# An FNet layer with an MLP on one core: the last step of the paired half, reordered

## The chip, the core and the metric

One NeuronCore of a Trainium2 chip runs the program. TensorE (PE) multiplies matrices into PSUM, VectorE (DVE), ScalarE (ACT) and GpSimd (POOL) work on vectors, and SyncE (SP) and GpSimd issue the transfers between HBM and the core's SBUF. The engines run side by side and wait for each other by semaphores; each works through its own instructions in the order in which the program gives them. The metric is the device time of one execution in microseconds (us): the median of the runs.

## The reference

```python
xn = _layernorm(x, axis=-1)                                   # x: 1 x 2048 x 640, float32
# _A_ref: real part of a DFT over the rows of a DFT over the columns
a = jnp.einsum("bsd,ed->bse", xn, dft_hid_re)
b = jnp.einsum("bsd,ed->bse", xn, dft_hid_im)
y = jnp.einsum("ts,bse->bte", dft_seq_re, a) - jnp.einsum("ts,bse->bte", dft_seq_im, b)
# _B_ref: w1 is 640 x 1536, w2 is 1536 x 640
h = _gelu(jnp.einsum("bsd,df->bsf", xn, w1) + b1)
m = jnp.einsum("bsf,fd->bsd", h, w2) + b2
return x + y + m
```

## The kernel before

All products are made in float32 out of two parts: a number is split into a high part (`high`, a copy on ACT) and a low part (`low`, a subtraction on DVE that needs the high part), and `product` issues three matmuls, high by high, high by low, low by high (lines 304 to 306). So a matmul needs both parts of what it reads, one from ACT and one from DVE.

The 2048 rows are four blocks of 512 (`NT` = 4). The MLP comes first. A *unit* is 128 of the 1536 hidden columns of one block: `hidden` (or, for two blocks at once, windows) sums it in a PSUM bank, `unit` applies the gelu, `split_unit` splits the result into a tile `hs`, and `output` multiplies it with w2 into five banks, 15 matmuls. Blocks 1 and 2 are done as a pair: `pair(k)`, k = 0 to 5, makes two units of each block by a Winograd-like scheme, in seven windows. Units of block 1 go on at once; those of block 2 are written to HBM (`gs`, from `keep`) and read back later (`load_unit`) into `units`, to be split and multiplied when block 2's turn comes. Two pairs of units, the last of blocks 1 and 2, are written out for later (`late_units`).

Beside each pair runs `beside_pair(k, at)`, called at seven places of the pair, in the order at = 2, 5, 6, 3, 8, 7, 4. It also turns the two matrices of the hidden DFT, wr and wi, into forms for a later stage, one chunk of 32 columns of each quarter at a time (five chunks, k = 1 to 5): `load_w` reads a chunk of both (SP), `turn_w` transposes it (DVE), and `prep_w(j, n)` forms it in three steps, n = 0, 1, 2 (`put_w`: high parts on ACT, low parts on DVE, additions on DVE, and a store `wit` on GpSimd for each form, eight stores in all). The raw chunk stands in places 0 and 1 of a four-row tile `row`, the turned one in places 2 and 3. The same four places take rows 12 to 15 of x (128 rows each, `load_x`), the fourth block's rows, for which the normalization is due: `ln_stats` (statistics on DVE), `ln_scale` (a root on ACT, five small operations on DVE), `ln_apply` (DVE). `put_z` then reorders the normalized rows by 16 transfers from SBUF to SBUF into a tile `z`, eight issued on SP and eight on GpSimd; `transpose_z` (DVE) and `prep_xt` (ACT, DVE) make of it the operand of block 3's hidden products.

After the last pair, block 2 is finished in a loop p = 2 to 11: in each turn up to p = 9 an `output` of 15 matmuls, the split of a unit that is used two turns on, and `between(p)`, the work beside it. From p = 10 on hidden products of block 3 come in. In `between`, `prep_w1` splits chunks of w1 for block 3, `load_w1` and `load_unit` read the next ones.

What sets the order is the program itself: it is written in order of each engine, by hand, and an engine that waits holds all that stands behind it in its queue. The places touched are in `beside_pair` for k = 5 (`LASTK`): `turn_w` at 6, `prep_w` steps at 3 and 7 (lines 1053 to 1061), `load_x` at 3 and 4, `split_unit` of units 0 and 1 at 7 and 4; and `between(2)` and `between(3)`, which hold the statistics, the scale, the applies and `put_z`. The seeds (`xab` from `banks`, line 1002 in the profile) are two sums of block 1 that ACT copies out of PSUM, into a place (`xab2`) that the last window of the pair reads before.

Of the kernel before, what the change touches and what calls it, by code (L numbers as in the profile page):

```python
# [27 lines left out]
def kernel(  # L28
# [55 lines left out]
    NF = F // P  # L84
# [104 lines left out]
    def high(h, s):  # L189
        nc.scalar.activation(h, s, AF.Copy)  # L190

    def low(l, s, h):
        nc.vector.tensor_tensor(l, s, h.bitcast(F32), op=ALU.subtract)  # L193
# [14 lines left out]
    def load_x(c, eng=nc.sync, k=None, home=None):  # L208

        slot[c] = c % NC if k is None else k  # L210
        xt[c] = (row_places if home is None else home)[:, slot[c]]
        eng.dma_start(xt[c], x[c * P : (c + 1) * P])

    def ln_stats(c):
        m = MV
        st = ST[1 if c == 0 else c % 2]
        half = D // 2
        for h in range(2):
            nc.vector.bn_stats(st[:, h, :], xt[c][:, h * half : (h + 1) * half])  # L219
        nc.vector.bn_aggr(m[:, slot[c], 0:2], st.rearrange("p a b -> p (a b)"))  # L220
# [37 lines left out]
    def zo_tile(name, shape=(P, NB, DQ), dtype=F32):  # L258
        return out_pool.tile(list(shape), dtype, tag="zo", bufs=1, name=name)
# [89 lines left out]
    def split_unit(g, a, fill=lambda k: None):  # L349
        hs = mr.tile([P, 2, TB], F32R, tag="hs", bufs=3, name=f"hs{g}")  # L350
        HT[g] = hs
        high(hs[:, 0], a)
        fill(1)
        low(hs[:, 1], a, hs[:, 0])
# [42 lines left out]
    def load_w(m, j):  # L397

        t = row_places[:, m].rearrange("p (e b) -> p e b", b=B)
        A["wraw", m] = t  # L400
        v = (wr, wi)[m].rearrange("(n r) d -> r n d", r=B)
        for q in range(Q):
            s0 = q * DQ + j * B
            nc.sync.dma_start(t[q * B : (q + 1) * B], v[:, :, s0 : s0 + B])
# [41 lines left out]
    def prep_w(j, k):  # L446

        (r1, r2, r4), (i1, i2, i4) = (
            (A["wt", m][:, : 2 * P], A["wt", m][:, 2 * P : 4 * P], A["wt", m][:, 4 * P :]) for m in range(2)
        )  # L450

        if k == 0:
            put_w(0, j, r1, r4)
            put_w(1, j, i1, i4)
            add(r4, r4, i4)
        if k == 1:
            put_w(6, j, i2, i4, True)
            add(i2, i2, r2)
            put_w(2, j, i2, r4)
            add(r2, r1, r2, ALU.subtract)  # L460
            add(r1, i2, r1, ALU.subtract)
            add(i1, i1, r1, ALU.subtract)
        if k == 2:
            put_w(3, j, r1)
            put_w(4, j, i1)
            put_w(5, j, r2)

    def add(dst, a, b, op=ALU.add):
        nc.vector.tensor_tensor(dst, a, b, op=op)  # L469
# [426 lines left out]
    def turn_x(key, z):  # L896
        transpose_z(key, Z[z], FORM_COLUMN[key[:2]] + int(key[2]))

    def split_x(key):
        split(*XF[key], zt.pop(key))  # L900
# [80 lines left out]
    def bias_sum(t, e):  # L981
        nc.scalar.activation(oacc[t][e], oacc[t][e], AF.Identity, bias=b2c[:, e : e + 1])

    def turn_sum(t, e, home=mr, tag="ab", biased=False):

        if not biased:
            bias_sum(t, e)
        yt = home.tile([P, TB], F32, tag=tag, bufs=2, name=f"ot{t}_{e}")
        nc.vector.transpose(yt, oacc[t][e])
        return yt  # L990

    def add_sum(t, e, yt):
        d = xo[t][:, :, e * B : (e + 1) * B]
        add(d, d, yt.rearrange("p (n i) -> p n i", i=B))

    def store_sums(t, *ks):
        for k in ks or range(len(YCOLS)):
            c0, c1 = YCOLS[k]
            nc.gpsimd.dma_start(ys[k][t], xo[t][:, :, c0:c1])
# [15 lines left out]
    LASTK = NF // 2 - 1  # L1015

    def beside_pair(k, at):

        if k == 0:

            if at == 5:
                bias_sum(0, 0)
                turn_x("t30", "a")
                turn_x("t31", "a")
                A["ot0"] = turn_sum(0, 0, rows, "yt", True)
                split_x("t30")
                split_x("t31")
            if at == 6:
                turn_x("t40", "a")
                turn_x("t41", "a")  # L1030
                split_x("t40")
                split_x("t41")
                bias_sum(0, 1)
                load_w(0, 0)
                load_w(1, 0)
            if at == 8:
                A["ot1"] = turn_sum(0, 1, rows, "yt", True)
            if at == 4:
                add_sum(0, 0, A["ot0"])
                add_sum(0, 1, A["ot1"])  # L1040
                store_sums(0, 0)
                bias_sum(0, 2)
            return
        j = k - 1
        if k == 1:
            if at == 2:
                add_sum(0, 2, turn_sum(0, 2, rows, "yt", True))
            if at == 5:
                finish(0, 3, 4)
                store_sums(0, 1, 2)  # L1050
            if at == 3:
                A["wst"] = zo_tile("wst", (P, NB * DQ), F32R)
        if at == (7 if k == 1 else 6):
            turn_w(0, j)
            turn_w(1, j)
        if k == 1:
            steps = {7: (0,), 4: (1,)}
        elif k == 2:
            steps = {5: (-1,), 7: (0, 1), 4: (2,)}
        elif k == LASTK:  # L1060
            steps = {3: (0,), 7: (1, 2)}
        else:
            steps = {3: (0,), 7: (1,), 4: (2,)}
        if at == (7 if k == 1 else 3) and j + 1 < ND:
            load_w(0, j + 1)
            load_w(1, j + 1)
        if k == LASTK and at == 3:
            load_x(12)
            load_x(13)
        for n in steps.get(at, ()):  # L1070
            prep_w(*((j - 1, 2) if n < 0 else (j, n)))
        if k == LASTK and at == 7:
            A["gs"] = place("xab3", (P, 5, TB), F32)
            for i in range(3, 6):
                load_unit(i)
            A["s1"] = place("xab2", (P, ND, TB), F32)
            split_unit(2 * NF, units[0])
        if k == LASTK and at == 2:
            for i in range(3):
                load_unit(i)  # L1080
        if k == LASTK and at == 4:
            load_x(14)
            load_x(15)
            for i in range(6, 8):
                load_unit(i)
            split_unit(2 * NF + 1, units[1])

    units = {}

# [66 lines left out]
    def between(p):  # L1156

        if p == 2:
            ln_stats(12)
            ln_stats(13)  # L1160
        if p == 3:
            ln_stats(14)
            ln_stats(15)
            ln_scale(NC)
            Z["z"] = zo_tile("z3")
            for c in range(3 * NC, 4 * NC):
                ln_apply(c)
            put_z(Z["z"], row_places, nc.gpsimd, nc.sync)
            new_xt(3)
        if p == 4:  # L1170
            with_bias(A["s1"][:, 0], 1, 2)
            keep_seed("x", A["s1"][:, :2])
        if p == 5:
            for e in range(2):
                less(A["s1"][:, 2 + e], 1, e, A["s1"][:, e])
            keep_seed("y", A["s1"][:, 2:4])
        for j in {6: (0,), 7: (1, 2), 8: (3, 4)}.get(p, ()):
            if j == 0:
                transpose_z("x30", Z["z"], 0)
            if j + 1 < ND:  # L1180
                transpose_z(f"x3{j + 1}", Z["z"], j + 1)
            prep_xt(f"x3{j}", j)
        if p == 10:
            open_place(*PLACES[3])
        if p == 11:
            open_place(*PLACES[2])
        for n in {2: (0,), 4: (1,), 5: (2,), 6: (3,), 7: (4,), 8: (5,), 9: (6, 7), 10: (8,), 11: (9,), 12: (10, 11)}.get(p, ()):
            prep_w1(AGAIN[n], 2 * NF + n)
            load_w1(2 * NF + 3 + n)
        if p in (2, 3):  # L1190
            load_unit({2: 8, 3: 9}[p])
        if p == 9:
            put_rows(3, row_places, nc.sync)
        if p == 10:
            A["s2"] = zo_tile("s2", (P, ND, TB))
            for k, key in ((0, "x"), (2, "us")):
                c0, c1 = SEEDS[key]
                nc.gpsimd.dma_start(A["s2"][:, k : k + c1 - c0], seeds[:, c0:c1])
# [57 lines left out]
    for p in range(2, 2 + NU):  # L1256
# [4 lines left out]
        elif p == NU + 1:  # L1261
# [3 lines left out]
            def fill(k):  # L1265
                for e in ((3,), (4, 2))[k]:
                    home, tag = (mr, "ab") if e == 2 else (rows, "yt")
                    kept[e] = with_bias(home.tile([P, TB], F32, tag=tag, bufs=2, name=f"s2_{e}"), 2, e)
# [691 lines left out]
```

## Time and profile before

| what | us |
|---|---|
| median of 3 runs | 857.02 (856.49 to 857.15) |
| the profiled execution | 856.42 |
| its span, first to last instruction | 854.6 |
| TensorE busy in it | 842.9 |
| VectorE busy | 685.9 |
| ScalarE busy | 372.0 |
| GpSimd busy | 80.7 |

A line of a timeline gives start, length, engine, line of the program, operation, out<-in by the program's names, shape and count; in brackets the idle time of the engine before it and what ended it. A line of stretches gives busy time by engine in one stretch, with the count of instructions, the granted clock of TensorE (1.00 is full), the share of time that the DMA engines were busy and what they moved. A line of DMA issues ends with the size in KB and the median time from issue to landing. TensorE's work is matmuls nearly throughout: the low digits of the page's slices are at its start and its end. The mean of a matmul there (387 to 390 ns) overlaps with the next, so the pace has to be read from starts. The last step of the pair, k = 5, lies between 181 and 200 us, and the loop over p follows it, to 245.

### The profile page before, as it was taken

The page shows a single profiled execution, that of the slowest core. Times are in us where ns is not written, and L with a number is a line of the kernel's source. Part 1 is how long each engine was busy: PE and PEld are TensorE (multiplying, and loading weights), DVE is VectorE, ACT ScalarE, POOL GpSimd, SP SyncE. Part 2 cuts the span into 40 slices and gives each one's busy share as a digit, 9 for nine tenths or more (in the row PEclk, how much of TensorE's full clock was granted, in tenths as well). Part 3 has the DMA queues.
Part 4 walks back from the last instruction along what each step waited for, and adds up shares of the span by engine and source line. Part 5 has one row for each costly group of instructions (what it writes and reads, how often), then busy time and mean ns, then how long its engine had stood idle before and what let it go on. Part 6 is the DMA issues. An engine that isn't in the chain of part 4 may idle for free.

```text
span 854.6 us, 10699 instructions
## 1 busy us (share of the span) xinstructions
PE 842.9 (99%) x3722; PEld 697.0 (82%) x3722; DVE 685.9 (80%) x912; ACT 372.0 (44%) x541; POOL 80.7 (9%) x147
## 2 busy tenths in 40 slices
PE   8999999999899999999999999999999999999998
PEld 7888888887688888888888888888888888888886
DVE  5979889757654778989898888889878888876895
ACT  6556657546254554534333343322324323244450
POOL 3340024223210000000000000000000000001012
PEclk9999999999999999999999999999999999999999
DMA  7995767878676959776843499474465899556353
GB/s 223 287 246 170 148 179 244 246 246 310 174 226 210 400 164 210 153 192 157 208 112 72 141 320 241 111 200 117 125 208 176 239 247 263 170 195 240 100 155 87
DMA packets 194054, 169.03 MB, mean 198 GB/s; under 512 B 57840, under 2 KB 164848, under 8 KB 193360
## 3 DMA queue, kind: packets, MB, share of 16 engines
q1 hardware_dynamic: 182528, 136.36, 60.4%
q0 software_dynamic: 9296, 31.47, 10.5%
q10 hardware_dynamic: 2176, 0.52, 0.3%
q8 instruction: 29, 0.48, 0.2%
q14 instruction: 25, 0.20, 0.1%
HBM read 117.71 MB, written 46.66 MB: 192 GB/s over the span
## 4 chain that ended last, share of the span: by engine, by line
PE 92%; issue 2%; DVE 2%; DMA 1%; ACT 1%; SPq 1%; POOL 1%; POOLq 0%; ACTq 0%
PE banks L305 27%; PE banks L306 27%; PE banks L304 27%; PE banks L326 10%; DMA g<-gs 1%; SPq L801 1%; DMA row<-in_A_x_dram 0%; POOL wit L444 0%; DVE st L219 0%; DVE hs L193 0%; DMA wit<-wst 0%; PE banks L707 0%; DVE row L469 0%; DVE row L235 0%; DVE xab L193 0%
## 5 line engine op out<-in xcount | busy, mean ns | idle before, releaser
L190 ACT ACTIVATE as<-r 128x1024 fp32r<-128x1024 f32 x80 | 85.0, 1062 | 170.3 <-PE banks L306 152.6
L306 PE MATMUL banks<-as,xab 128*128 128x512 f32 (+1 forms) x389 | 150.5, 387 | 0.0
L305 PE MATMUL banks<-as,xab 128*128 128x512 f32 (+1 forms) x389 | 150.5, 387 | 0.0
L304 PE MATMUL banks<-as,xab 128*128 128x512 f32 (+1 forms) x389 | 150.5, 387 | 0.0
L193 DVE TENSOR_TENSOR as<-r,as 128x1024 fp32r<-128x1024 f32 x80 | 97.1, 1215 | 38.1 <-ACT as L190 38.0
L304 PE MATMUL banks<-as,xc 128*128 128x512 f32 x234 | 91.0, 389 | 0.0
L305 PE MATMUL banks<-as,xc 128*128 128x512 f32 x234 | 91.0, 389 | 0.0
L306 PE MATMUL banks<-as,xc 128*128 128x512 f32 x234 | 91.0, 389 | 0.0
L304 PEld LDWEIGHTS banks<-as,xab 128*128 128x128 f32 x389 | 73.0, 188 | 14.9
L305 PEld LDWEIGHTS banks<-as,xab 128*128 128x128 f32 x389 | 73.0, 188 | 14.9
L306 PEld LDWEIGHTS banks<-as,xab 128*128 128x128 f32 x389 | 73.0, 188 | 14.8
L190 ACT ACTIVATE as<-rt 128x1024 fp32r<-128x1024 f32 (+1 forms) x36 | 36.5, 1015 | 78.1 <-PE banks L306 59.3
L326 PE MATMUL banks<-xt,xab 128*128 128x512 f32 x240 | 56.6, 390 | 0.0
L326 PEld LDWEIGHTS banks<-xt,xab 128*128 128x128 f32 x240 | 45.0, 188 | 9.3
L193 DVE TENSOR_TENSOR hs<-ab,hs 128x512 fp32r<-128x512 f32 x34 | 23.4, 688 | 35.3 <-ACT hs L190 34.8
L304 PEld LDWEIGHTS banks<-as,xc 128*128 128x128 f32 x234 | 43.9, 188 | 9.1
L305 PEld LDWEIGHTS banks<-as,xc 128*128 128x128 f32 x234 | 43.9, 188 | 9.1
L306 PEld LDWEIGHTS banks<-as,xc 128*128 128x128 f32 x234 | 43.9, 188 | 9.1
L193 DVE TENSOR_TENSOR as<-rt,as 128x1024 fp32r<-128x1024 f32 (+1 forms) x36 | 41.5, 1153 | 9.0 <-ACT as L190 9.0
L304 PE MATMUL banks<-hs,xc 128*128 128x512 f32 x120 | 46.8, 390 | 1.7 <-ACT hs L190 1.7
L305 PE MATMUL banks<-hs,xc 128*128 128x512 f32 x120 | 46.8, 390 | 0.2 <-DVE hs L193 0.2
L306 PE MATMUL banks<-hs,xc 128*128 128x512 f32 x120 | 46.7, 389 | 0.0
(301 smaller groups left out, 1678.6 us busy)
## 6 DMA issues: line engine op xcount, KB each, us to landing
raw<-in_A_dft_seq_re_dram SPq DMA_DIRECT2D x64, 256.0 KB, 5.3
raw<-in_A_dft_seq_im_dram SPq DMA_DIRECT2D x64, 256.0 KB, 5.2
w1r<-in_B_w_dram SPq DMA_DIRECT2D x144, 80.0 KB, 3.4
wit<-wst POOLq DMA_DIRECT2D x15, 384.0 KB, 4.3
wit<-wst POOLq DMA_DIRECT2D x20, 256.0 KB, 4.4
forms_ab<-xab SPq DMA_DIRECT2D x4, 1280.0 KB, 7.5
xab<-wit SPq DMA_DIRECT2D x13, 384.0 KB, 4.5
row<-xn SPq DMA_DIRECT2D x14, 320.0 KB, 5.1
```

The lines of the kernel that those rows point to most:

```text
L190: nc.scalar.activation(h, s, AF.Copy)
L193: nc.vector.tensor_tensor(l, s, h.bitcast(F32), op=ALU.subtract)
L304: nc.tensor.matmul(acc, wh, mh, start=first, stop=False, skip_group_check=goes_on)
L305: nc.tensor.matmul(acc, wh, ml, start=False, stop=False, skip_group_check=goes_on)
L306: nc.tensor.matmul(acc, wl, mh, start=False, stop=last, skip_group_check=goes_on)
L326: nc.tensor.matmul(acc, W1[i][:, a, j * P : (j + 1) * P], XT[j][:, b], start=n == 0, stop=n == len(steps) - 1)
L801: engines[q % len(engines)].dma_start(z[q * B : (q + 1) * B].rearrange("r (c a) d -> r a c d", a=NC)[:, a], rows[a * B : (a + 1) * B, :, q ...
```

## The change

In the last step of the pair the turn of the last chunk moves from place 6 to place 2, and the three steps of its forming from 3, 7, 7 to 5, 6, 3. Rows 12 and 13 are loaded at 5 instead of 3, rows 14 and 15 at 3 instead of 4, right behind the third step, which is the last to read their places. Unit 0 of block 2 is split at 3 instead of 7, unit 1 at 7 instead of 4. The statistics of rows 12 and 13 are taken at 8 and those of rows 14 and 15 at 4, both inside the pair, and no longer in `between(2)` and `between(3)`; the scale, the applies and the reordering come in `between(2)` instead of `between(3)`.

```diff
-        if at == (7 if k == 1 else 6):
+        if at == {1: 7, LASTK: 2}.get(k, 6):
             turn_w(0, j)
             turn_w(1, j)
...
         elif k == LASTK:
-            steps = {3: (0,), 7: (1, 2)}
+            steps = {5: (0,), 6: (1,), 3: (2,)}
...
-        if k == LASTK and at == 3:
+        if k == LASTK and at == 5:
             load_x(12)
             load_x(13)
         for n in steps.get(at, ()):
             prep_w(*((j - 1, 2) if n < 0 else (j, n)))
+        if k == LASTK and at == 3:
+            load_x(14)
+            load_x(15)
+            split_unit(2 * NF, units[0])
+        if k == LASTK and at == 8:
+            ln_stats(12)
+            ln_stats(13)
         if k == LASTK and at == 7:
             A["gs"] = place("xab3", (P, 5, TB), F32)
             for i in range(3, 6):
                 load_unit(i)
             A["s1"] = place("xab2", (P, ND, TB), F32)
-            split_unit(2 * NF, units[0])
+            split_unit(2 * NF + 1, units[1])
...
         if k == LASTK and at == 4:
-            load_x(14)
-            load_x(15)
             for i in range(6, 8):
                 load_unit(i)
-            split_unit(2 * NF + 1, units[1])
+            ln_stats(14)
+            ln_stats(15)
...
         if p == 2:
-            ln_stats(12)
-            ln_stats(13)
-        if p == 3:
-            ln_stats(14)
-            ln_stats(15)
             ln_scale(NC)
             Z["z"] = zo_tile("z3")
             for c in range(3 * NC, 4 * NC):
```

On DVE, from the third step of the forming on (`wst` is a form, `hs` a unit's split, `g` a unit read back, `zc` a unit of the pair, `st` and `mv` statistics), stands before:

```order
L193 TENSOR_TENSOR wst_4_1959<-row,wst_4_1959 128x256
L193 TENSOR_TENSOR wst_4_1963<-row,wst_4_1963 128x256
L193 TENSOR_TENSOR wst<-row,wst 128x256
L193 TENSOR_TENSOR hs_1975<-g_1863,hs_1975 128x512
L193 TENSOR_TENSOR hs_2009<-g_1865,hs_2009 128x512
L193 TENSOR_TENSOR hs_2030<-g_1867,hs_2030 128x512
L219 BN_STATS st_92<-row 128x6 x2
```

And in the change, at the same step:

```order
L469 TENSOR_TENSOR ab_1902<-ab_1902,banks 128x512
L193 TENSOR_TENSOR wst_4_1941<-row,wst_4_1941 128x256
L193 TENSOR_TENSOR wst_4_1945<-row,wst_4_1945 128x256
L193 TENSOR_TENSOR wst<-row,wst 128x256
L193 TENSOR_TENSOR hs_1954<-g_1865,hs_1954 128x512
L469 TENSOR_TENSOR zc_1880<-zc_1880,banks 128x512
L219 BN_STATS st_92<-row 128x6 x2
L220 BN_AGGR mv<-st_92 128x2
L219 BN_STATS st_93<-row 128x6 x2
L220 BN_AGGR mv<-st_93 128x2
L193 TENSOR_TENSOR hs_1986<-g_1867,hs_1986 128x512
```

The third step and the first unit's split (`hs_1954`) now stand ahead of the addition into `zc`, which stood between the first and the second step before, and the statistics of rows 12 and 13 stand ahead of the second unit's split.

A little further on DVE, around the applies (line 235), stands before:

```order
L193 TENSOR_TENSOR xab_2012<-w1r_1607,xab_2012 128x640
L193 TENSOR_TENSOR hs_2063<-xab_1970,hs_2063 128x512
L219 BN_STATS st_92<-row 128x6 x2
L220 BN_AGGR mv<-st_92 128x2
L219 BN_STATS st_93<-row 128x6 x2
L220 BN_AGGR mv<-st_93 128x2
L227 TENSOR_SCALAR mv<-mv 128x4
```

And in the change, with the unit that is used third (`hs_2042`) in front:

```order
L219 BN_STATS st_92<-row 128x6 x2
L220 BN_AGGR mv<-st_92 128x2
L219 BN_STATS st_93<-row 128x6 x2
L220 BN_AGGR mv<-st_93 128x2
L193 TENSOR_TENSOR hs_2042<-g_1869,hs_2042 128x512
L227 TENSOR_SCALAR mv<-mv 128x4
```

The w1 chunk and the fourth unit's split, which stood ahead of the statistics of rows 14 and 15, come behind the applies now.

On SP, from the units' loads on, stands before (x3 is three transfers in a row; `row` is rows 12 to 15, `z` the reordered rows, `w1r` a chunk of w1):

```order
L1094 DMA g_1867<-gs 128x512
L212 DMA row<-in_A_x_dram 128x640 x2
L1094 DMA xab_1970<-gs 128x512 x3
L212 DMA row<-in_A_x_dram 128x640 x2
L1094 DMA xab_1970<-gs 128x512 x2
L282 DMA w1r_2041<-in_B_w_dram 32x5x128 x4
L1094 DMA g_2046<-gs 128x512
L801 DMA z_2078<-row 32x4x160 x8
L1094 DMA g_2100<-gs 128x512
```

And in the change:

```order
L1100 DMA g_1869<-gs 128x512
L212 DMA row<-in_A_x_dram 128x640 x4
L1100 DMA xab_1981<-gs 128x512 x5
L801 DMA z_2051<-row 32x4x160 x8
L282 DMA w1r_2075<-in_B_w_dram 32x5x128 x4
L1100 DMA g_2080<-gs 128x512
L1100 DMA g_2100<-gs 128x512
```

All four rows now go ahead of the five unit loads into `xab`, and `z` goes ahead of one w1 chunk and one unit load.

## The prediction

> **What bounds the kernel now.** I read the page first, then the busy time by stretch, then TensorE's timeline in the two stretches where it is not full, then the lines of the other engines just ahead of those gaps.
>
> ```profile
> span 854.6 us, 10699 instructions
> PE 842.9 (99%) x3722; PEld 697.0 (82%) x3722; DVE 685.9 (80%) x912; ACT 372.0 (44%) x541; POOL 80.7 (9%) x147
> ```
>
> TensorE is the bound: 842.9 of 854.6 us. A change that leaves the matmuls as they are can gain only what TensorE loses by waiting or by a lower clock. The stretches show where that is (columns: length, PE busy with count, PEld, DVE, ACT, POOL, granted clock, DMA share, GB/s).
>
> ```profile
> 181.03:200.07 19.04, 19.04 (x85) 15.58 (x83) 9.50 (x23) 8.23 (x19) 6.25 (x13) 1.00 0.93 321
> 200.07:203.47 3.40, 1.44 (x5) 0.86 (x5) 2.38 (x6) 3.22 (x7) 2.52 (x6) 1.00 0.80 251
> 203.47:226.39 22.92, 22.92 (x102) 18.77 (x100) 14.28 (x32) 7.66 (x13) 6.44 (x12) 1.00 0.87 271
> 226.39:231.50 5.11, 1.73 (x7) 1.08 (x7) 4.49 (x7) 2.77 (x5) 0.00 (x0) 1.00 0.47 134
> 231.50:235.10 3.60, 3.60 (x10) 2.80 (x9) 3.57 (x7) 2.05 (x5) 0.00 (x0) 0.53 0.31 80
> 323.50:600.00 276.50, 276.50 (x1221) 228.96 (x1220) 241.75 (x221) 104.80 (x110) 0.00 (x0) 1.00 0.70 170
> ```
>
> The first row is the last step of the paired half (k = 5); TensorE is full in it. The last row gives the pace: 276.50 / 1221 = 0.2265 us for each matmul. In between are two holes, after 200.07 and after 226.39, and behind the second one the clock is at half (0.53). TensorE's own lines give their size:
>
> ```profile
> 198.03 0.39 PE L304 MATMUL banks<-as,w1f 128*128 128x512 f32 x1
> 199.84 0.39 PE L306 MATMUL banks<-xab,w1f 128*128 128x512 f32 x1
> 201.95 0.49 PE L304 MATMUL banks<-hs,xc 128*128 128x512 f32 x1 [1.73 <-ACT hs L190]
> 202.68 0.50 PE L305 MATMUL banks<-hs,xc 128*128 128x512 f32 x1 [0.23 <-DVE hs L193]
> 205.76 0.39 PE L306 MATMUL banks<-hs,xc 128*128 128x512 f32 x1
> 226.16 0.39 PE L306 MATMUL banks<-hs,r 128*128 128x512 f32 x1
> 229.49 0.49 PE L304 MATMUL banks<-hs,r 128*128 128x512 f32 x1 [2.93 <-ACT hs L190]
> 238.53 0.39 PE L306 MATMUL banks<-hs,r 128*128 128x512 f32 x1
> ```
>
> First hole: from 199.84 to 205.76 are 15 matmuls, 15 x 0.2265 = 3.40 us of work in 5.92, so 2.52 us lost. Second: from 226.16 to 238.53 are 30 matmuls, 6.80 us of work in 12.37, so 5.57 lost, the half clock included. Together 8.09 us. Both holes wait for a unit's split (`hs`: high part on ACT, low part on DVE).
>
> **First hole: what the change does to it.** The first output of block 2 needs unit 0 split. These lines of DVE and ACT carry it now:
>
> ```profile
> 187.12 0.85 DVE L409 STREAM_TRANSPOSE row<-row 128x640 f32<-128x640 f32 x1 [0.98 <-DMA row<-in_A_dft_hid_im_dram]
> 192.18 0.69 DVE L469 TENSOR_TENSOR ab<-ab,banks 128x512 f32<-128x512 f32 x1 [4.21 <-PE banks L306]
> 195.50 0.69 DVE L469 TENSOR_TENSOR zc<-zc,banks 128x512 f32<-128x512 f32 x1 [0.18 <-PE banks L306]
> 199.29 1.33 DVE L469 TENSOR_TENSOR row<-row 128x256 f32<-128x256 f32 x3
> 200.70 1.17 DVE L193 TENSOR_TENSOR wst<-row,wst 128x256 fp32r<-128x256 f32 x3
> 201.93 0.69 DVE L193 TENSOR_TENSOR hs<-g,hs 128x512 fp32r<-128x512 f32 x1
> 188.08 0.60 ACT L335 ACTIVATE ab<-banks 128x512 f32<-128x512 f32 x1 [0.82 <-PE banks L306]
> 192.90 0.72 ACT L346 ACTIVATE ab<-ab,b1c 128x512 f32<-128x512 f32 x1 [4.21 <-DVE ab L469]
> 193.53 1.11 ACT L190 ACTIVATE wst<-row 128x256 fp32r<-128x256 f32 x4
> 196.86 0.40 ACT L190 ACTIVATE wst<-row 128x256 fp32r<-128x256 f32 x1
> 200.25 1.13 ACT L190 ACTIVATE wst<-row 128x256 fp32r<-128x256 f32 x3 [1.34 <-issue]
> ```
>
> The second transposition stays where it is on DVE, behind the same add and the same landing: it ends at 187.97. DVE and ACT then sit idle (both 4.21) although the chunk lies ready. The change fills that hole. Behind 187.97 ACT has about two of the first step's four highs (half of 1.11) and the term (0.60): the second step starts at 189.1. Second step in before: from 196.86 to 199.29 + 1.33 = 200.62, 3.76 us; so its adds end at 192.9. The unit's add (0.69) is queued behind them on DVE: 193.5, some 0.7 later than now; its gelu (0.72): 194.3. Third step and split in before: from 200.25 to 201.93 + 0.69 = 202.62, 2.37 us; so unit 0 is split at 196.7, against 200.07 where TensorE wants it. **Gain 2.52**, cover 3.4.
>
> What is queued behind: the add into `zc` (195.50 now) goes behind the split's low part, 196.7 to 197.4. It frees the bank into which the last window starts at 198.03: 0.6 to spare, and TensorE does not wait unless the chain slips by more. Edits with one answer: the two transpositions, loads of rows 12 and 13 (behind the same three unit loads on SyncE) and the chunk's eight stores on GpSimd only go earlier; for these stores only the third step's last form waits, whose buffer is that of the first form: written out from about 189 on, wanted at about 195, and such a store takes 2.9 (first row of the next fence).
>
> **Second hole.** Here DVE waits for the reordered rows 12 to 15 (`z`), and the next split stands behind it in the queue.
>
> ```profile
> wit<-wst POOLq DMA_DIRECT2D x2, 384.0 KB, 2.9
> row<-in_A_x_dram SPq DMA_DIRECT2D x2, 320.0 KB, 4.9
> row<-in_A_x_dram SPq DMA_DIRECT2D x2, 320.0 KB, 6.9
> 208.72 0.88 DVE L219 BATCH_NORM_STATS2 st<-row 128x6 f32<-128x320 f32 x2
> 211.00 0.17 DVE L227 TENSOR_SCALAR mv<-mv 128x4 f32<-128x4 f32 x1
> 212.17 2.18 DVE L235 TENSOR_SCALAR row<-row,mv 128x640 f32<-128x640 f32 x4
> 201.81 1.25 ACT L1002 ACTIVATE xab<-banks,b2c 128x512 f32<-128x512 f32 x2
> 206.84 1.28 ACT L226 ACT_TABLE_LOAD   x1
> L801 SPq DMA_DIRECT2D z<-row x8: 593/673/1277, 214.4 to 219.6; - x8
> 226.91 1.30 DVE L263 STREAM_TRANSPOSE ztx<-z 128x512 f32<-128x512 f32 x2 [7.97 <-DMA g<-gs]
> 229.69 0.69 DVE L193 TENSOR_TENSOR hs<-xab,hs 128x512 fp32r<-128x512 f32 x1
> 233.54 0.69 DVE L193 TENSOR_TENSOR hs<-g,hs 128x512 fp32r<-128x512 f32 x1
> 228.82 0.61 ACT L190 ACTIVATE hs<-xab 128x512 fp32r<-128x512 f32 x1
> ```
>
> (The releaser is named `g`, the last landing near; the transposition reads `z`.) From the first `z` issue, 214.4, to the transposition, 226.91, are 12.5 us. Rows 14 and 15 go out when the third step has read their places, about 0.7 ahead of the split's end: 196.0, where the same step's lows end at 200.70 + 1.17 = 201.87 in before. By the two DMA rows (the loads of rows 12, 13, then of 14, 15) they land 4.9 to 6.9 later, 200.9 to 202.9. Statistics of two tiles take 211.00 - 208.72 = 2.3: those of 12 and 13 run from 197.4 to 199.7, unit 1's low part to 200.4, those of 14 and 15 end at 203.2 (early landing) to 204.1 (late: one tile is left), and unit 2's low part (0.7) at 203.9 to 204.8. ACT has its own chain: the two seeds (1.25) go into a place that the last window still reads, so from 200.1; a gelu 0.7, unit 2's high part 0.6 and the table load 1.28 bring it to 204.0, about the same. From 211.00 to the end of the applies, 212.17 + 2.18 = 214.35, are 3.35. So `z` starts at 207.4, **7.0 earlier**; the bounds are 207.2 and, with another us for the traffic, 209.
>
> With no first hole TensorE comes to the output that stalled at 200.07 + 7 x 3.40 = 223.87 (15 matmuls for each of seven outputs). Its split, moved by 7.0: high part 228.82 + 0.61 - 7.0 = 222.4 (1.4 to spare); low part 230.38 - 7.0 = 223.4, wanted with the second matmul at 224.1 (0.7 to spare). One output on, 227.27: low part 234.23 - 7.0 = 227.2, wanted at 227.5 (0.3). So the hole closes, by a small margin: **gain 5.57**. The cover is thin: from half a us of lateness on, each further us of `z` costs TensorE a us, and that sets the upper end.
>
> On SyncE's queue `z` now also goes ahead of the four pieces of one w1 chunk and one unit load. For `z` that can only help. The chunk is formed on ACT just ahead of the split whose output stalled, so a late chunk delays it as a late `z` does; I take nothing for it, since the chunk is issued right behind `z` and read after `z`'s first two transpositions (1.30) and a split; the bound is 1 us, and it lies in the same rival as late `z`.
>
> By the Trainium skill, "DMA: Bandwidth & Descriptors", Anatomy of one DMA (about 2 us and then 436 GB/s), an estimate for the 16 pieces of 80 KB is 4.9 us, and `z` would have 7 us to spare; the trace has 12.5 for it, and the trace decides.
>
> **Sum.** The profiled execution took 856.42 with a span of 854.6; 856.42 - 2.52 - 5.57 = 848.3. The median of the runs, 857.02, lies 0.6 above it: 848.9, and I forecast 849.0, as the margins at the second hole leave about 0.1. It is a floor too, since nothing else is freed.
>
> **Rivals.** *Late `z`.* For it: DMA share is 0.93 in the pair's stretch, and the stores moved forward there compete with rows 14 and 15 for it; margins are 0.3 to 0.7. If `z` takes 14 us, or starts at 209, TensorE waits 1 to 2.5 us: 850 to 851.5. A wait near 3 brings the half clock again (half of 3.6 us, 1.7): up to 853.6. The row shows no loss of clock behind the first hole's 1.73 and a loss behind 2.93. The skill's "TensorE: Matmul & The Clock Gate", Part 1, puts the fall behind an idle window of about 3.4 us; by that alone such a rest would cost only itself, 852.0.
>
> *Crowded pair.* The `zc` add slips past 198.03: say a first-step store holds the third step's buffer for 2 us more. Then the last window waits 1 to 2: 850 to 851. Against: 0.6 to spare, and 5 us of age for the store.
>
> *Slower.* DVE works in order: the statistics of rows 14 and 15 now stand ahead of unit 2's low part, which TensorE wants at 200.07 + 2 x 3.40 = 206.9. If row 15 lands late, that part is ready 1.9 behind the landing (a tile 1.15, the part 0.7), TensorE waits there, and the half clock adds 1.7; `z` is then covered by the wait itself. It eats the whole 8.09 and another 1.7 from a landing at 213 on, 17 us after the issue; at 215 the time is 857.0 - 8.1 + 10.0 + 1.7 = 860.6. The slowest such landing shown is 6.9.
>
> *Nothing.* Some other wait takes both places, for instance the seeds or the table load in front of block 2: 856 to 858. The columns of ACT (44% busy) speak against it.
>
> **Chances.** Both holes closed, within 0.7: 0.64. Late `z`: 0.22 without the half clock, 0.04 with it. Crowded pair: 0.05. Slower: 0.02. Nothing: 0.03. A change within 0.2% (1.7 us) can't be told from none here. So faster 0.95, same 0.03, slower 0.02. The range runs from 848.4 (the floor less 0.5, as the lowest of the runs, 856.49, lies 0.5 below their median) to 852.0, which holds the forecast, the crowded pair and nearly all of late `z`.
>
> **What would show it.** Right: TensorE full from 200.07 on, unit 0's low part at about 196.7, `zc` at 197, rows 14 and 15 issued near 196, `z` issued near 207.4, its transposition near 220, clock 1.00 throughout 226 to 235. Wrong: TensorE waiting for `zc` ahead of 200; a wait for `hs` at 224 or 227; the transposition's line later than 221; or DVE idle ahead of its statistics beyond 203.

## The result, and the profile after

The change takes 849.90 us, the median of six runs (849.36 to 851.72), beside 857.05 for the kernel before in the same rounds (856.49 to 858.62). The ratio is 0.9918, with a 95% interval of 0.9905 to 0.9931: 7.15 us faster. The profiled execution took 850.62, 0.7 above the median, with a span of 848.8. The page's first lines:

```profile
span 848.8 us, 10702 instructions
PE 841.9 (99%) x3722; PEld 696.3 (82%) x3722; DVE 686.3 (81%) x912; ACT 372.5 (44%) x541; POOL 80.8 (10%) x147
```

Every engine is busy about as long as before, and the span is 5.8 shorter: 4.8 of it are time in which TensorE was not busy (11.7 before, 6.9 now), the other 1.0 is its busy time, for the same 3722 matmuls. The stretches after, with the columns as before (length, PE, PEld, DVE, ACT, POOL, clock, DMA share, GB/s):

```profile
181.25:200.30 19.05, 19.05 (x85) 15.66 (x84) 12.68 (x31) 10.30 (x24) 8.66 (x16) 1.00 1.04 346
200.30:207.10 6.80, 6.80 (x32) 5.63 (x31) 3.98 (x11) 3.74 (x6) 1.08 (x2) 1.00 1.01 387
207.10:213.00 5.90, 5.20 (x23) 3.64 (x22) 5.76 (x14) 4.45 (x8) 2.14 (x4) 1.00 0.41 130
...
224.00:231.50 7.50, 7.34 (x32) 5.37 (x31) 7.34 (x12) 4.88 (x9) 0.89 (x2) 1.00 0.67 193
231.50:235.00 3.50, 3.50 (x17) 2.92 (x16) 2.30 (x4) 1.26 (x3) 0.20 (x1) 1.00 0.91 273
```

TensorE is full through 200, where the first hole was, and the clock is 1.00 in every row, the last one included, where it was 0.53 before: the half clock is gone. Two things are new. The pair's stretch and the one behind it have the DMA engines busy throughout (1.04 and 1.01, against 0.93 and then 0.80 to 0.87 before), and there is a small hole in the third row, where before had none. TensorE's starts show what is left, one matmul being due 0.2265 behind the other:

```profile
200.14 0.39 PE L306 MATMUL banks<-xab,w1f 128*128 128x512 f32 x1
200.37 0.39 PE L304 MATMUL banks<-hs,xc 128*128 128x512 f32 x1
...
207.17 0.39 PE L304 MATMUL banks<-hs,xc 128*128 128x512 f32 x1
207.62 0.50 PE L305 MATMUL banks<-hs,xc 128*128 128x512 f32 x1
...
210.93 0.39 PE L304 MATMUL banks<-hs,xc 128*128 128x512 f32 x1
211.95 0.50 PE L305 MATMUL banks<-hs,xc 128*128 128x512 f32 x1 [0.64 <-DVE hs L193]
...
225.46 0.39 PE L304 MATMUL banks<-hs,r 128*128 128x512 f32 x1
225.90 0.50 PE L305 MATMUL banks<-hs,r 128*128 128x512 f32 x1
...
229.25 0.39 PE L304 MATMUL banks<-hs,r 128*128 128x512 f32 x1
229.75 0.50 PE L305 MATMUL banks<-hs,r 128*128 128x512 f32 x1
```

From the last window (200.14) into block 2 (200.37) there is no gap. Four waits remain in this execution, each for a unit's low part on DVE: 0.22 at 207, 0.79 at 211, 0.21 and 0.27 at 225 and 229, with some 0.1 more behind each, 1.9 in all. The two holes of before had 8.1. In a second profiled execution of the same kernel (experiment 11) only the last two waits are there, so the first two are not a fixed part of the change.

DVE's lines say why the low parts at 207 and 211 were late:

```profile
187.83 0.85 DVE L409 STREAM_TRANSPOSE row<-row 128x640 f32<-128x640 f32 x1 [1.47 <-DMA row<-in_A_dft_hid_im_dram]
...
196.85 0.69 DVE L193 TENSOR_TENSOR hs<-g,hs 128x512 fp32r<-128x512 f32 x1
197.46 0.68 DVE L469 TENSOR_TENSOR zc<-zc,banks 128x512 f32<-128x512 f32 x1
201.16 0.89 DVE L219 BATCH_NORM_STATS2 st<-row 128x6 f32<-128x320 f32 x2 [1.98 <-DMA row<-in_A_x_dram]
203.96 0.89 DVE L219 BATCH_NORM_STATS2 st<-row 128x6 f32<-128x320 f32 x2 [1.11 <-DMA row<-in_A_x_dram]
205.84 0.89 DVE L219 BATCH_NORM_STATS2 st<-row 128x6 f32<-128x320 f32 x2 [0.75 <-DMA row<-in_A_x_dram]
206.89 0.68 DVE L193 TENSOR_TENSOR hs<-g,hs 128x512 fp32r<-128x512 f32 x1
208.38 2.18 DVE L235 TENSOR_SCALAR row<-row,mv 128x640 f32<-128x640 f32 x4
...
211.21 1.29 DVE L193 TENSOR_TENSOR hs<-xab,hs 128x512 fp32r<-128x512 f32 x2
222.33 1.30 DVE L263 STREAM_TRANSPOSE ztx<-z 128x512 f32<-128x512 f32 x2 [5.51 <-DMA w1r<-in_B_w_dram]
```

Three times DVE stands idle in front of statistics until a row has landed (1.98, 1.11, 0.75). The third unit's low part (206.89) is queued behind the last of them, the fourth's (211.21) behind the applies. The loads of the rows, among the issues between 189 and 199 (KB, us to landing):

```profile
row<-in_A_x_dram SPq DMA_DIRECT2D x4, 320.0 KB, 8.0
```

And who issues `z`, from the view of that tile (the last two figures are the first and the last issue):

```profile
L801 SPq DMA_DIRECT2D z<-row x8: 594/608/1432, 210.6 to 215.7; - x8
```

The four rows take 8.0 us from issue to landing, where the two pairs of loads in before took 4.9 and 6.9. `z` is issued at 210.6, 3.8 earlier than before.

### The profile page after: what moved, and what is told of

Read it like the earlier page. It is cut to its first block, busy times and chain, and to the rows that moved or that the text cites. A ratio compares the mean times of both kernels' runs of the same rounds, so it can differ in the third digit from the quotient of the medians.

```text
span 848.8 us, 10702 instructions
## 1 busy us (share of the span) xinstructions
PE 841.9 (99%) x3722; PEld 696.3 (82%) x3722; DVE 686.3 (81%) x912; ACT 372.5 (44%) x541; POOL 80.8 (10%) x147
## 4 chain that ended last, share of the span: by engine, by line
PE 93%; DMA 3%; issue 1%; SPq 1%; DVE 1%; POOL 1%; ACT 0%; POOLq 0%; ACTq 0%
PE banks L305 27%; PE banks L306 27%; PE banks L304 27%; PE banks L326 10%; DMA row<-in_A_x_dram 1%; PE banks L691 1%; DMA w1r<-in_B_w_dram 1%; DMA wit<-wst 1%; SPq L801 1%; POOL wit L444 0%; SPq L282 0%; PE banks L707 0%; DVE row L235 0%; DVE hs L193 0%; DVE st L219 0%
```

## The experiments

The theory: each of the two holes was a chain that came late, first the forming and unit 0's split, then rows, statistics and `z`; both chains are now early enough, and what is left comes from the rows, whose landing the busy DMA engines delay. Rivals: one of the parts does it all; the earlier stores are what slows the rows; or something else than the rows' time makes `z` late. Every kernel computes all of the reference and none leaves work out; two move more than they need: experiment 3 stores some forms twice, and experiment 12 copies 1 MB that nobody reads.

**1. The turn, the forming and the splits alone; rows and statistics as before.**

```diff
-        if k == LASTK and at == 5:
+        if k == LASTK and at == 3:
             load_x(12)
             load_x(13)
...
+            load_x(14)
+            load_x(15)
...
+            ln_stats(12)
+            ln_stats(13)
+        if p == 3:
+            ln_stats(14)
+            ln_stats(15)
```

> The kernel before with the turn, the forming and the splits of units 0 and 1 moved as in the change, rows 12 to 15 and their statistics as before. Theory: the two holes are in series and the second hangs on the landing of rows 14 and 15, not on TensorE. The first hole (2.5 us) closes, TensorE comes to the second that much sooner and waits that much longer unless z comes sooner as well: 857.0 if z is first issued at 214.4 as before, less by as much as it is issued sooner; I expect 212 to 214 and 854.5 to 857. Rival (the holes add up, each worth its own size): 854.5 with z issued at 214.4.

Measured: 855.59, ratio 0.9982 (0.9973 to 0.9992). TensorE's line at its second hole:

```profile
228.33 0.51 PE L304 MATMUL banks<-hs,r 128*128 128x512 f32 x1 [4.59 <-ACT hs L190]
```

The first hole is gone, and the second has grown: TensorE arrives 2.8 earlier (its last matmul starts at 223.35 instead of 226.16) and waits 4.59 where it waited 2.93. `z` itself is issued at 212.6 instead of 214.4, and its transposition comes 1.2 earlier (225.75 instead of 226.91). So of the 1.5 us that the kernel gains most is what `z` gained, and the closed hole of 2.5 by itself gives next to nothing. The gains of two holes in series are not independent: what the first gives, the second takes, until its own chain moves too.

This run also shows what the earlier stores do to the rows. Rows 12 and 13 are loaded where they were before (issues between 189 and 199), and what moved around them is the turn, the forming with its stores, and the splits:

```profile
row<-in_A_x_dram SPq DMA_DIRECT2D x2, 320.0 KB, 7.7
```

They took 4.9 in the kernel before. So the earlier stores are at least part of what makes the rows late.

**2. The change with the splits of units 0 and 1 at their old places.**

```diff
         if k == LASTK and at == 3:
...
-            split_unit(2 * NF, units[0])
...
         if k == LASTK and at == 7:
...
-            split_unit(2 * NF + 1, units[1])
+            split_unit(2 * NF, units[0])
...
         if k == LASTK and at == 4:
...
+            split_unit(2 * NF + 1, units[1])
```

> The change with the splits of units 0 and 1 left at their old places (7 and 4), so behind the statistics of rows 12 and 13 on VectorE. Theory: VectorE works in order and row 13 lands at 201.1, so unit 0's low part comes at about 202.2 and the first hole opens again with 2 to 2.5 us; z is issued near 210.6 as in the change, TensorE comes later to it and finds no wait there: 851 to 852. Rival (the earlier forming alone closes the first hole, since all its work is done by 197): 849.5 to 850.3.

Measured: 850.04, ratio 0.9916 (0.9901 to 0.9931): the same as the change. The time expected was missed. The wait did come back, as its lines on DVE and TensorE show:

```profile
199.70 0.89 DVE L219 BATCH_NORM_STATS2 st<-row 128x6 f32<-128x320 f32 x2 [1.09 <-DMA row<-in_A_x_dram]
200.75 0.64 DVE L193 TENSOR_TENSOR hs<-g,hs 128x512 fp32r<-128x512 f32 x1
...
201.45 0.50 PE L305 MATMUL banks<-hs,xc 128*128 128x512 f32 x1 [1.04 <-DVE hs L193]
```

Unit 0's low part stands behind row 13's statistics and TensorE waits 1.04. The waits at 207 and 211 are gone here, as they are in the second execution of the change, and those for `z` come to 0.6, read from TensorE's starts, where that execution had 1.4: TensorE comes there later. The earlier splits by themselves earn nothing that these runs show. The wait is paid at whichever split first stands behind rows that have not landed.

**3. The stores of the last chunk's first two steps issued twice, to load the DMA engines** (lines of the program from 446 on are one higher in this kernel).

```diff
-            nc.gpsimd.dma_start(wits[w][j][:, :, c0:c1], t.bitcast(F32))
+            for _ in range(2 if last and w in (0, 1, 2, 6) else 1):
+                nc.gpsimd.dma_start(wits[w][j][:, :, c0:c1], t.bitcast(F32))
```

> The change with the last chunk's stores of the first two steps' forms (five of eight, 1.5 MB) issued twice each. Theory: what is left of the second hole comes from rows 12 to 15 landing late (7 to 10 us after issue) beside these stores; twice the stores put the landing of row 15 some 3 to 4 us later, z is first issued at 213 to 215 and the time is 852 to 856. Rival (it comes from VectorE, which has the statistics in front of the splits): z at 210.6, 849.5 to 850.5.

Measured: 864.35, ratio 1.0084 (1.0068 to 1.0099), far more than expected, and by other ways:

```profile
199.37 0.42 ACT L190 ACTIVATE wst<-row 128x256 fp32r<-128x256 f32 x1 [5.11 <-DMA wit<-wst]
...
201.68 0.80 PE L304 MATMUL banks<-as,w1f 128*128 128x512 f32 x1 [3.64 <-DVE zc L470]
```

ACT waits 5.11 for the buffer that a store still reads, the add into `zc` behind it is late, and the last window waits 3.64: the crowded pair, as the prediction described it, at a price that the change itself does not pay (0.06 there). Later `z` waits too (first issued at 223.3), since its tile lies where some of those forms stood, and TensorE waits another 7.02, at 237.67, for the split that stands behind its transposition. As a test of the rows it says nothing: they were issued later, and their statistics, from 201.54 to 205.2, ended no later than in the change.

**4. The seeds' stores written later in the program** (the two calls of `keep_seed` moved to `p == 8`).

> The change with the two stores of seeds x and y (512 KB each) moved from p = 4 and 5 to p = 8, behind the transfers of z and out of their time. Theory: they share the DMA engines with the last pieces of z; without them z is transposed 10 us after its first issue instead of 11.7, the waits at 225 to 230 (0.7 us together) go: 849.0 to 849.4. Rival (z is bound by its own issue on SyncE, 6.5 us, and its small pieces): no difference, 849.9.

Measured: 849.97, ratio 0.9917 (0.9902 to 0.9932). This tested nothing: the stores are issued by GpSimd, and nothing else of GpSimd's stood between the old and the new place, so its order stayed the same and the stores still went out right behind its half of `z` (from 214.5). It serves as a second measurement of the change.

**5. The seeds' two stores on SyncE, at `p == 8`.** GpSimd issues these two stores of 512 KB right behind its half of `z`.

```diff
-            keep_seed("x", A["s1"][:, :2])
...
-            keep_seed("y", A["s1"][:, 2:4])
...
+        if p == 8:
+            for key, k in (("x", 0), ("y", 2)):
+                nc.sync.dma_start(seeds[:, SEEDS[key][0] : SEEDS[key][1]], A["s1"][:, k : k + 2])
```

> The change with the stores of seeds x and y issued on SyncE at p = 8, behind the loads of four w1 chunks there (the run before it, with these stores moved in the program alone, left GpSimd's own order as it was and so tested nothing). Theory: the two stores, 1 MB, take DMA time from the last pieces of z; without them z is transposed about 2 us sooner behind its first issue (9.5 to 10.5 instead of 11.7), and the waits at 225 to 230, 0.7 together, go: 849.0 to 849.5. Rival (z is bound by its own issue and pieces): 11.7 as before, 849.9.

Measured: 849.28 (848.89 to 849.78), ratio 0.9910 (0.9893 to 0.9926). Its issue of `z`:

```profile
L801 SPq DMA_DIRECT2D z<-row x8: 594/624/1377, 209.2 to 214.3; - x8
```

The transposition, on DVE's timeline:

```profile
217.66 1.30 DVE L263 STREAM_TRANSPOSE ztx<-z 128x512 f32<-128x512 f32 x2 [2.25 <-DMA w1r<-in_B_w_dram]
```

The releaser named is a load that landed close by, as in the change; the transposition reads `z`, which experiments 7, 9 and 10 name there.

And the stretch 196 to 236:

```profile
196.00:236.00 40.00, 40.00 (x178) 32.99 (x177) 27.12 (x53) 20.67 (x33) 7.71 (x15) 1.00 0.82 259
```

TensorE is busy in all 40.00 us, as it was in none of the kernels above. From the first issue of `z` to the transposition it is now 8.5, in the change 11.7; from its last issue (214.3, and 215.7 in the change) 3.4 and 6.6. So some 3 us of the time of `z` come from the seeds' stores beside its last pieces. The other profiles agree: wherever GpSimd issues these stores behind `z`, the transposition comes 11.7 to 13.2 behind the first issue, and 8.5 to 9.0 in the four kernels where it does not (experiments 5, 7, 9 and 10). The issues between 213.8 and 216.5 in the change show the neighbours (KB each, us to landing):

```profile
seeds<-xab POOLq DMA_DIRECT2D x2, 512.0 KB, 5.5
z<-row SPq DMA_DIRECT2D x4, 80.0 KB, 4.7
```

In the kernel of this experiment the same four pieces, the last that SyncE issues, took 3.7; the last two of them took 3.3, and 5.6 in the change. The time came out as expected, but its lead over the change, 0.6, is within the intervals.

**6. Rows 14 and 15 loaded from ACT's queue.**

```diff
-            load_x(14)
-            load_x(15)
             split_unit(2 * NF, units[0])
+            load_x(14, nc.scalar)
+            load_x(15, nc.scalar)
```

> The change with rows 14 and 15 loaded from ScalarE's own queue, right behind unit 0's high part, instead of SyncE's. Theory: what made z late (issued at 210.6, where 207.4 was forecast) is the landing of rows 14 and 15 at 203.9 and 205.8, held up in SyncE's queue behind the units and rows 12 and 13; on a queue of their own they land at 201 to 203, z is first issued at 208 to 209, the waits of units 2 and 3 at 207 and 211 (1.2 together) go and half of those at 225 to 230: 848.6 to 849.3. Rival (all DMA engines are full there, share 0.95 to 1.03, so another queue gains nothing): row 15 lands at 205 or later, 849.9.

Measured: 850.42 (849.37 to 850.57), ratio 0.9918 (0.9904 to 0.9933). No time is gained. The loads between 189 and 199 in its profile:

```profile
row<-in_A_x_dram ACTq DMA_DIRECT2D x2, 320.0 KB, 7.0
row<-in_A_x_dram SPq DMA_DIRECT2D x2, 320.0 KB, 7.9
```

This profile is of the fastest of its executions (849.37). A queue of their own saves these two rows at most 1 us out of 8, and in experiment 7, where they are loaded in the same way, they took 8.3. The waits at 207 and 211 are gone and those for `z` stay (0.44 at 224.62), but the second execution of the change shows the same without this edit. So at most a small part of the rows' 8 us is SyncE's queue.

**7. Experiments 5 and 6 together.**

> Both edits, rows 14 and 15 on ScalarE's queue and the two seeds on SyncE. Theory: no wait of TensorE is left between 198 and 240; the time is the floor, 848.0 to 848.9. Rival (each edit without effect): 849.9.

Measured: 849.20 (848.32 to 849.28), ratio 0.9904 (0.9890 to 0.9919). The time is above what was expected, and one wait is left (0.42, for unit 3's low part at 210.95). Not to be told from experiment 5: with the seeds out of the way the rows' queue gives nothing that can be seen.

**8. The change with the scale, the applies and `put_z` at their old place.** In `between`, `if p == 2:` is `if p == 3:` again for that block.

> The change with the scale, the applies and the reordering back at p = 3, the statistics as in the change. Theory: on VectorE a w1 chunk and unit 3's split come in front of the applies, and on SyncE a w1 chunk and a unit in front of z; z is first issued 1.5 to 2 us later (212 to 212.6); the wait for unit 3 at 211 (0.9) goes, and TensorE waits 2.5 to 3.5 us more for z: 851.4 to 852.6, more by 1.7 if the clock falls. Rival (the earlier statistics bring all of the gain, since the rows set the time): 849.5 to 850.3.

Measured: 853.23, ratio 0.9955 (0.9941 to 0.9970). Its issue of `z`:

```profile
L801 SPq DMA_DIRECT2D z<-row x8: 593/620/1352, 211.4 to 216.5; - x8
```

TensorE's two waits:

```profile
226.99 0.50 PE L304 MATMUL banks<-hs,r 128*128 128x512 f32 x1 [1.73 <-ACT hs L190]
227.93 0.50 PE L305 MATMUL banks<-hs,r 128*128 128x512 f32 x1 [0.44 <-DVE hs L193]
```

And the stretch of these waits, with the one behind it:

```profile
224.87:228.20 3.33, 1.16 (x4) 0.46 (x3) 3.23 (x6) 2.30 (x4) 0.00 (x0) 1.00 0.26 75
228.20:231.50 3.30, 3.30 (x9) 2.53 (x9) 3.27 (x6) 2.30 (x4) 0.00 (x0) 0.53 0.37 104
```

`z` is issued 0.8 us later than in the first profile of the change and 2.4 later than in its second (experiment 11), and its transposition, at 224.42, comes 2.1 and 3.0 later. That costs 3.3 us: 1.73 and 0.44 of waiting, and then the half clock (0.53), for which the expectation had allowed. The late-`z` rival is real, and the change stands only a little ahead of it.

**9. The kernel before, with only the seeds' stores moved to SyncE** (the edit of experiment 5 alone).

> The kernel before, with the seeds x and y stored from SyncE at p = 8 and nothing else. Theory: the second hole hangs on the landing of z alone, and the two stores take some 3 us of its time; z is issued at 214.4 as before and transposed 8.5 to 9 us later, at 223, ahead of 226.4 where TensorE wants the split: the second hole (5.5) goes, the first stays: 851.3 to 852.2. Rival (z has to start earlier, as in the change): 855 or more.

Measured: 851.90 (851.46 to 852.84), ratio 0.9940 (0.9928 to 0.9953). Its issue of `z`:

```profile
L801 SPq DMA_DIRECT2D z<-row x8: 593/702/1157, 213.8 to 219.2; - x8
```

The transposition on DVE, and TensorE at what is left of the second hole:

```profile
222.78 1.31 DVE L263 STREAM_TRANSPOSE ztx<-z 128x512 f32<-128x512 f32 x2 [4.43 <-DMA z<-row]
...
230.15 0.50 PE L305 MATMUL banks<-hs,r 128*128 128x512 f32 x1 [0.16 <-DVE hs L193]
```

`z` is issued 0.6 earlier than in before and transposed 4.1 earlier (222.78 instead of 226.91), so 3.5 of it belong to the stores. The first hole stays (1.73 at 201.50), the second one is all but gone. Beside the kernel before in the same rounds (856.74) the two stores moved give 4.84 us, where the whole reordering, run beside them in experiment 11, gives 6.80.

**10. Experiment 1 with the seeds' stores moved.**

> The turn, forming and splits moved as in the change, rows and statistics as before, the seeds x and y on SyncE at p = 8. Theory: the first hole goes by the early split; z, issued at 212.6 as in the run with the split alone and transposed 8.5 to 9 us later at 221.3, leaves a wait of 0 to 1.2 at 223.9: 849.2 to 850.5. Rival (the earlier rows and statistics are needed): 854 or more.

Measured: 850.75 (850.42 to 851.24), ratio 0.9926 (0.9913 to 0.9938), a little over what was expected, with `z` issued at 213.6, a us later than expected. Beside experiment 5 (849.28), the earlier rows, statistics and `z` are worth about 1.5 once the seeds are out of the way.

**11. The change once more**, beside the next kernel.

> The change as it is, beside the others on one chip: 849.5 to 850.5, rows 14 and 15 landing 7 to 9 us after issue, z issued at 209.5 to 211.

Measured: 849.94 (849.29 to 850.74), ratio 0.9916 (0.9903 to 0.9930). In its profile the rows take 7.6 and `z` goes out at 209.0, 1.6 earlier than in the first one: such a step varies by that much between executions of one kernel. TensorE does not wait at 207 and 211 here; what is left is the wait for `z`, transposed at 221.43:

```profile
224.95 0.50 PE L305 MATMUL banks<-hs,r 128*128 128x512 f32 x1 [0.43 <-DVE hs L193]
...
228.80 0.50 PE L305 MATMUL banks<-hs,r 128*128 128x512 f32 x1 [0.15 <-DVE hs L193]
```

Read from TensorE's starts, these two waits with what follows them come to 1.4 us.

**12. The change with 1 MB more to move:** a copy from HBM to HBM that nobody reads, issued by ACT in place 6 of the pair.

```diff
+    spare_rows = dram.tile([4, P, TB], F32, name="spare_rows")
...
+        if k == LASTK and at == 6:
+            nc.scalar.dma_start(spare_rows, gs[0:4])
```

> The change with one copy of 1 MB from HBM to HBM into a tensor that nobody reads, issued from ScalarE's own queue behind the second step of the forming, at about 192. Theory: the DMA engines are full from 189 to 207 (shares 0.95 to 1.03), so any other transfer puts off rows 14 and 15, by 2.5 to 5 us (1 MB read and written at some 390 GB/s); z is issued at 212 to 215 and the time is 851.5 to 855. Rival (the rows wait for their own queue, not for the engines): rows and time as in the change.

Measured: 853.97, ratio 0.9958 (0.9942 to 0.9974). Its loads between 189 and 199:

```profile
row<-in_A_x_dram SPq DMA_DIRECT2D x4, 320.0 KB, 12.9
```

And DVE and TensorE (the lines of the program are one higher in this kernel):

```profile
203.35 0.89 DVE L220 BATCH_NORM_STATS2 st<-row 128x6 f32<-128x320 f32 x2 [7.14 <-DMA row<-in_A_x_dram]
206.43 0.64 DVE L194 TENSOR_TENSOR hs<-g,hs 128x512 fp32r<-128x512 f32 x1
...
207.13 0.79 PE L306 MATMUL banks<-hs,xc 128*128 128x512 f32 x1 [3.61 <-DVE hs L194]
```

The rows now take 12.9, DVE stands 7.14 in front of row 12's statistics, and unit 1's low part, queued behind them, comes at 206.43: TensorE waits 3.61, and the half clock follows (0.51 from 207.1 to 213.2). This is the mechanism of the prediction's slower rival, at unit 1 instead of unit 2, though the time stays below that of the kernel before. More bytes in flight delay the rows by 4.9, where a queue of their own (experiment 6) gave at most 1.

## Why the prediction was right, and where it was off

*First hole, 2.52.* Right, and by the steps given, with one price off. The transposition ended 0.7 later than in before (188.68), unit 0's low part at 197.54 instead of 196.7, with 2.8 of the cover of 3.4 left; TensorE runs on into block 2. The stores of 384 KB, taken at 2.9 each, needed 8.2 (the median of the three issued between 186 and 200), so ACT had to wait for the buffer that the crowded pair was about:

```profile
195.88 0.42 ACT L190 ACTIVATE wst<-row 128x256 fp32r<-128x256 f32 x1 [0.43 <-DMA wit<-wst]
```

The cover took that up. The `zc` add ended at 198.14 and cost the last window 0.06 at most; its cover of 0.6 was used up, no more.

*Second hole, 5.57.* Right in kind only: the half clock is gone, but a wait of 0.7 (first profile) or 1.4 (second) is left, at the two matmuls whose margins were given as 0.7 and 0.3. Three of the prediction's four signs of being wrong appeared: waits for `hs` at the two matmuls meant, the transposition later than 221 (222.33 and 221.43), and DVE idle ahead of its statistics beyond 203. What came is the late-`z` rival without the half clock, at its low end. The median of 849.90 lies 0.2 beyond the "within 0.7" of the main branch and just below the 850 where that rival began; that it lies so near the forecast of 849.0 is in part luck.

*The landing of rows 14 and 15: the mis-sized term.* "They land 4.9 to 6.9 later" was read from loads of before. The change itself moves the chunk's stores and all four rows into one stretch, and in 189 to 207 the DMA engines are now busy throughout. The two lines are that stretch before and after:

```profile
189.00:207.00 18.00, 16.04 (x70) 12.74 (x69) 10.16 (x26) 9.43 (x22) 6.79 (x12) 1.00 0.84 297
```

```profile
189.00:207.00 18.00, 18.00 (x81) 14.77 (x80) 11.72 (x32) 9.10 (x19) 6.79 (x12) 1.00 1.00 368
```

The share goes from 0.84 to 1.00 and the rows from 4.9 and 6.9 to 8.0; experiment 1, where the stores have moved and the rows have not (share 0.98), has 7.7 for rows 12 and 13, and experiment 12, with more bytes, gets 12.9. It is the traffic that does it. The statistics therefore ended at about 206.9 instead of 204.1, and `z` went out at 210.6 (209.0 in the second profile of the same kernel) instead of 207.4, past or at the upper bound of 209.

*What that cost.* In the second profile, what the late-`z` rival's own sum gives: `z` at 209.0, TensorE not late, 1.4 of waiting. In the first profile `z` was issued 3.2 later than forecast and transposed 2.4 later (it took 11.7 instead of 12.5), and that cost only 0.7, for a reason that the prediction missed: the same late rows held the splits of units 2 and 3 on DVE and cost TensorE about 1.2 at 207 and 211, so it came later to the second hole as well. Unit 3's split behind the applies was not priced at all; for unit 2 only the landing from 213 on was. Together with 0.7 at 225 and 229 that is 1.9 of the 2.3 by which the first profiled execution (850.62) lies above the sum for it (848.3); the median lies 1.0 above its own (848.9). Experiment 2 shows the same from the other side: let TensorE wait 1.04 at unit 0, and the waits for `z` are 0.6, though `z` was transposed 0.5 later than in the second profile of the change (221.93 and 221.43).

*The 12.5 us of `z`.* It was taken as the time of the transfer. Experiments 5 and 9 show that 3 to 3.5 us of it come from the two stores of seeds behind it, which were in no term. By the Trainium skill, "DMA: Bandwidth & Descriptors", Anatomy of one DMA, a fit for one transfer on GpSimd's path, the estimate for these bytes as one transfer was 4.9. The runs, with 16 pieces from two queues, have 11.7, and 8.5 without the seeds, of which 5.1 pass from the first issue to the last. The prediction was right to go by the trace; asking what stood in the trace's number would have shown a cheaper change.

*Rivals.* Late `z` came without the half clock; with it, it is 0.8 to 2.4 us of issue away (experiment 8). The prediction's threshold was too kind: it had no loss of clock behind 1.73, a loss behind 2.93, and put the fall near 3. In experiment 8 waits of 1.73 and 0.44 were enough. Nor does the Trainium skill's "TensorE: Matmul & The Clock Gate", Part 1, with an idle window of about 3.4 us, hold as a rule for one gap: there TensorE was still busy for 1.16 of the 3.33 us. The crowded pair and the slower rival have their mechanisms (experiments 3 and 12), each with a price only under traffic that the change does not make.

*Open.* Whether experiment 6 is worth anything: its profile loses less than the first one of the change, its median does not show it. Why the issue of `z` varies by 1.6 us between executions of one kernel. The lead of experiments 5 and 7 over the change, 0.6 to 0.7, is within the intervals; with 0.06 us of waiting left in the profile of experiment 5 there is nothing more for this part of the kernel to give.

## What to carry to other kernels

A DMA's time read from one trace holds only for the traffic around it there: before a load is moved, read the DMA share of the stretch into which it goes, and add the bytes that the same change moves there. When a transfer is late, look first at what big store is issued beside it on another queue and is not urgent; here moving two such stores was worth about 0.7 of what the whole reordering was worth. Gaps in series on one engine don't add up: closing the first hands its time to the next, and anything that waits for a load should not stand, in an in-order queue, ahead of what the bottleneck wants next.

## What the runs showed of the hardware

Loads of 320 KB took 4.9 and 6.9 us from issue to landing (medians of two pairs) where the DMA engines were busy 0.84 of the stretch, 8.0 at 1.00, and 12.9 with another 1 MB in flight. Two stores of 512 KB on GpSimd's queue delayed the last of 16 small pieces, issued ahead of or with them on SyncE's queue: those two took 5.6 to 6.0 us and 3.3 without the stores, and the tile was in use 3 to 3.5 us sooner without them. The clock fell to about half, for some 3.3 us, behind waits of 1.73 and 0.44 us in experiment 8, and stayed full behind 1.73 and 0.23 in the kernel before and behind 0.61 and 0.44 in experiment 10; what separates these was not tested.
